# Attention over a cache and a gated layer on one core: values' products at the landing, output chunks shared by three engines

## The chip, the core and the metric

The kernel runs on one core of a Trainium2 chip: TensorE (PE), VectorE (DVE), ScalarE (ACT) and GpSimd (POOL) compute, SyncE (SP) issues nearly all transfers from HBM into SBUF. The metric is the device time of one execution in microseconds, the median of three runs.

## The reference

One token of decoding. `x` (576 numbers) is normalised; attention with 32 heads runs over a cache of 8192 keys and values of 128 numbers each, and a gated layer of width 4608 stands beside it.

```python
xn = _layernorm(x)
q = xn @ wq                                          # 32 heads x 128
p = softmax((q . k_cache) * 128 ** -0.5)             # 8192 per head
o = p . v_cache                                      # per head
a = concat(o) @ wo                                   # 4096 -> 576
g = xn @ W_gate;  g = g * (g > 0)
b = (g * (xn @ W_up)) @ W_down                       # 4608 -> 576
return x + a + b
```

All arrays are float32. Keys and values are 134 MB each, the four weights about 51 MB together.

## The kernel before

**Storage.** Most of SBUF is `slots`, three places of 128 x 16384 numbers: two for keys (`KEYS`), one for values (`VALUES`). A load of keys or values (`kk[i]`, `vv[i]`) fills one place with two heads (a pair; there are `NP` = 16). The weights of q, gate and up (`wl`, four tiles of 26 chunks of 576 columns) pass through the same places first, and the weights of both output products (`wod`, 68 chunks of 576 columns: 36 of `W_down`, 32 of `wo`) last. Pair p (from 1) has the keys `kk[p-1]` and the values `vv[p-1]`.

**Order.** Nothing is scheduled by a planner: `add(engine, f, waits, to)` appends to an engine's list, with the semaphores that it waits for and the one that it raises; `loop` and `done` enclose a hardware loop whose counter sets the waits' values. `emit` writes the lists. Each engine runs its list in order.

**Stages.** (1) x is broadcast to all partitions by a TensorE product with ones, normalised into `xp` (PSUM) and `xb` (SBUF). (2) The chunks of `wl` are multiplied with x and summed: most by VectorE (`dot`), 12 of each of the last three tiles by GpSimd (`others`) and ScalarE (`total`). The sums are columns of `dots`. (3) The loop over pairs. For each head VectorE multiplies the keys by q (`product`, in place) and adds up along a head's 128 numbers (`sums`), then takes the maximum per partition (`mr`). TensorE brings the maxima across partitions into `pm` (`maxima`), VectorE makes the negative bias `nb` (`bound`), ScalarE the exponentials (`soft`, with the sum of p into `L`), TensorE the products with the values (`values(0)`, `values(1)`, 16 matmuls each, into `bo`) and the sum of `L` over partitions (`pl`); ScalarE copies `bo` out (`oc`), four small matmuls turn it into `ot`, and `close` divides and writes columns of `coef`. A query for the next pair: GpSimd spreads columns of `dots` on a diagonal (`diagonals` into `dq`), and TensorE broadcasts it into `qb` (`query`). In this kernel each bias is computed half a pair late, between the next head's product and its sums, and the query stands between `values(0)` and `values(1)`. (4) The output: 62 chunks are added by VectorE alone into `acc` (60 in the loop at L380, two at L388), the last six (`LAST`) go through TensorE into `po` with `acc` itself; the two halves of the row are copied and stored.

**The queue on SP.** Keys of the next pair are asked for when the place is free (`sumb`) and the keys before have landed (`kland`); values when those of the pair before are used (`vb`). Increments on SP (`passed`, L157) tell other engines of a landing; `chunks` counts rounds of output chunks that are ready. An increment waits on the same queue as the loads do, so it also waits for whatever stands before it there.

Of the kernel before, what the change touches and what calls it, by code (L numbers as in the profile page):

```python
# [15 lines left out]
P = 128  # L16
# [21 lines left out]
LOADS = (27, 5, 4, 4, 4, 4, 4, 4, 4, 2, 2, 2, 1, 1)  # L38
ROUNDS = 15
LAST = 6  # L40

HEADS = {"tensor": 0, "vector": 128, "scalar": 128}


class Program:
# [21 lines left out]
    def loop(self, engine, start, end, step=1):  # L67
        self.lists[engine].append((start, end, step))
# [4 lines left out]
    def emit(self, engine):  # L73
        eng = getattr(self.nc, engine)
        lines = iter(self.lists[engine])
        if engine in HEADS:
            with self.nc.Fori(0, 1, 1, engines=[ENGINES[engine]], head_slot={ENGINES[engine]: HEADS[engine]}):
                self.run(engine, eng, lines, None)
        else:
            self.run(engine, eng, lines, None)  # L80

    def run(self, engine, eng, lines, counter):
        for line in lines:
            if line is None:
                return
            if len(line) == 3:
                with self.nc.Fori(*line, engines=[ENGINES[engine]]) as i:
# [12 lines left out]
def build(nc, x, wl, kk, vv, wod, out):  # L100
# [26 lines left out]
    acc = sb("acc", [P, D])  # L127
# [12 lines left out]
    mr = sb("mr", [P, 1])  # L140
    nb = [sb(f"nb{i}", [P, 1]) for i in range(2)]
    L = sb("l", [P, G])
    rl = sb("rl", [P, G])

    bo, bb, bm, bt, po = [bank(f"bank{i}") for i in range(5)]
    xp = nc.alloc_psum_tensor("xp", [P, 1024], F32).ap()[:, :D]
    qb = bb[:, :G * DH].rearrange("p (h d) -> p h d", d=DH)
    pm = bm[:, :P]
    ot = bt[:, :G]
    pl = bt[:, 8:8 + G]  # L150
# [34 lines left out]
    places, f = [], 0  # L185
    for k, n in enumerate(LOADS):
        if k == 1:
            load(VALUES, vv[NP - 1], (("vb", NP - 1),), "vland")
        waits = {0: (("sumb", NP - 1),), 1: (("sumb", NP),), 8: (("vb", NP),)}.get(k, ())
        load(slots[:, OUT + f * D:][:, :n * D], wod[:, f * D:(f + n) * D], waits, f"do{k}")  # L190
        f += n
        places += [k] * n
    assert f == H + FC
    ready = 0
    for k in range(max(places[:4 * ROUNDS]) + 1):
        full = sum(places[4 * m + 3] <= k for m in range(ROUNDS))
        if full > ready:
            passed(f"do{k}", "chunks", (full - ready))
            ready = full
# [9 lines left out]
    add("gpsimd", lambda e: e.memset(acc, 0.0), (), "acc0")  # L209
    add("gpsimd", lambda e: e.memset(pzs, 0.0), (), "pz0")  # L210
    def diagonals(pairs):
        for k in pairs:
            waits = (("q", k),) if k else (("dots", A + 3), ("scaled", 1))
            add("gpsimd", lambda e, k=k: e.tensor_mul(dq, scaled[:, None, :].to_broadcast([P, G, P]),  # L214
                                                      dots[:, G * k:G * k + G, None].to_broadcast([P, G, P])),
                waits, "dq" if k > 1 else "dq0")

    for k in range(3):
# [4 lines left out]
        if k == 0:  # L223
            diagonals(range(2))
    diagonals(range(2, NP))
    for k in range(2):
        add("gpsimd", lambda e: e.sem_inc(pr.sems["dq"], 1), (("q", NP + k),))

# [3 lines left out]

    add("scalar", lambda e: e.dma_start(xr, x), (), "dx", 16)
    mm((("dx", 16), ("ones", 1)), None, 0, xp[:, :512], ones[:1, :].to_broadcast([1, P]), xr[:, :512])
    mm((), "bx", 1, xp[:, 512:], ones[:1, :].to_broadcast([1, P]), xr[:, 512:])
# [5 lines left out]
    add("vector", lambda e: e.memset(pm, 0.0), (), "pmb", 1)  # L241
    add("vector", lambda e: e.memset(bt[:, :16], 1.0), (), "ot", 1)
    add("scalar", lambda e: e.activation(row, xp, AF.Copy, accum_out=sm[:, 0:1]), (("bx", 1),), "ln")  # L243
    add("vector", lambda e: e.tensor_scalar_mul(sm[:, 1:2], sm[:, 0:1], -1.0 / D), (("ln", 1),), "lv")  # L244
    add("vector", lambda e: e.tensor_scalar_add(xp, xp, sm[:, 1:2]), (("lv", 1),), "lv")
# [45 lines left out]

    def sums(m):
        x = "ab"[m]
        def f(e, i):
            k3 = slots[:, ds(at(i) + m * SK, SK)].rearrange("p (c d) -> p c d", d=DH)
            return e.reduce_sum(s2[m], k3, axis=AX.X)  # L296
        add("vector", f, (), f"sum{x}", 1)
        add("vector", lambda e, i: e.reduce_max(mr, s2[m], axis=AX.X), ((f"sum{x}", lambda i: i),), f"mr{x}", 1)  # L298


    def bound(m, value, waits=()):
        x = "ab"[m]
        add("vector", lambda e, *i: e.tensor_reduce(nb[m], pm, axis=AX.X, op=ALU.max, negate=True), waits + ((f"pm{x}", value),), f"nb{x}", 1)  # L303

    def close(value, place):
        add("vector", lambda e, *i: e.reciprocal(rl, pl), (("ot", value),), "rl", 1)
        add("vector", lambda e, *i: e.tensor_mul(coef[:, place(*i)], ot, rl), (("rl", value),), "os", 1)

    pr.loop("vector", 1, NP + 1)
# [8 lines left out]
    bound(1, NP + 1)  # L318
    add("vector", lambda e: e.tensor_copy(acc[:1, :], xr), (("acc0", 1), ("dx", 16)), "mrb")
    hh, gate, up = coef[:, :FC], dots[:, H:H + FC], dots[:, H + FC:]  # L320
    add("vector", lambda e: e.tensor_scalar(hh, gate, 0.0, None, op0=ALU.is_gt), (("sums", 3 * OTHERS), ("os", NP)), "mulb", 1)
    add("vector", lambda e: e.tensor_mul(hh, hh, gate), (("mulb", NP + 1),), "mra", 1)
    add("vector", lambda e: e.tensor_mul(hh, hh, up), (("mra", NP + 1),), "accd", 1)


    def soft(h):
        r, i = h // G, h % G
        waits = ((f"nb{'ab'[i]}", (r + 1 + i)),) + (((("va", r),) if r else (("pz0", 1),)) if i == 0 else ())
        add("scalar", lambda e: e.activation(pz[:, i, :, 4 * G - 4:4 * G], s2[i].rearrange("p (c b) -> p c b", b=4), AF.Exp,  # L329
                                             bias=nb[i], scale=1.0, accum_out=L[:, i:i + 1]), waits, f"exp{i}", 1)  # L330

    for r in range(NP):
        if r == 0:
            soft(0)
            soft(1)
        if r + 1 < NP:
            soft(G * r + G)
        add("scalar", lambda e: e.copy(row[:, :512], bo), (("vb", r + 1),), "oc", 1)  # L338
        if r + 1 < NP:
            soft(G * r + G + 1)  # L340
# [5 lines left out]
    def maxima(m, value):  # L346
        x = "ab"[m]
        mm(((f"mr{x}", value),), f"pm{x}", 1, pm, mr.to_broadcast([P, P]), ident)

    def values(i, waits):  # L350
        for c in range(C // 4):
            j = c % 4
            end = c == C // 4 - 1
            mm(waits if c == 0 else (), f"v{'ab'[i]}" if end else None, 1, bo[32 * j:32 * j + 4 * G, :],
# [3 lines left out]
    query((("dq0", 1),))  # L358
    maxima(0, 1)
    query((("dq0", 2), ("mulb", 1)))  # L360
    maxima(1, 1)
    pr.loop("tensor", 1, NP + 1)
    mm((("exp1", lambda i: i + 1),), None, 0, pl, ones.to_broadcast([P, P]), L)
    maxima(0, lambda i: i + 1)
    values(0, (("vland", lambda i: i * 16),))
    query((("dq", lambda i: i), ("mulb", lambda i: i + 1)))
    values(1, ())
    for b in range(4):
        mm((("oc", lambda i: i),) if b == 0 else (), "ot" if b == 3 else None, 1, ot, row[:, b * P:(b + 1) * P],
           sel.rearrange("p (i b) -> p i b", b=4)[:, :, b], b == 0, b == 3)  # L370
    maxima(1, lambda i: i + 1)
# [3 lines left out]

    pr.loop("vector", 1, ROUNDS + 1)
    for m in range(4):
        def chunk(e, i, m=m):
            c = slots[:, ds(i * (4 * D) + (OUT - 4 * D + m * D), D)]
            return e.scalar_tensor_tensor(out=acc, in0=c, scalar=coef[:, ds(i * 4 + (m - 4), 1)], in1=acc, op0=ALU.mult, op1=ALU.add)  # L380
        waits = ((f"acc{'dabc'[m]}", lambda i: i),) if m else (("chunks", lambda i: i), ("accd", lambda i: i))
        add("vector", chunk, waits, f"acc{'abcd'[m]}", 1)
    pr.done("vector")

    close(NP + 1, lambda: slice(FC + H - G, FC + H))
    for n, k in enumerate(range(4 * ROUNDS, H + FC - LAST)):
# [58 lines left out]
```

## Time and profile before

| | |
|---|---|
| median of three runs | 810.74 us (809.76 to 811.58) |
| the profiled execution's own time | 811.15 us |
| its span | 809.4 us |
| TensorE, share of the span | 27% |
| VectorE | 83% |
| ScalarE, GpSimd | 7% each |
| bytes moved by the queue on SP | 319.17 MB |

A time in the profile is in us from the start of the span; a line number (L289) is one of the kernel before. In a row of the timeline stand the start, the duration, the engine, the line, the operation with output and inputs, how many were merged, and in brackets the idle time before it with what ended it. In a row of stretches stand the busy time and count of PE, its weight loads, DVE, ACT and POOL, then the granted clock of TensorE, the transfers' share and GB/s.

### The profile page before, as it was taken

To read this page: it belongs to the slowest core of one execution; us is meant where nothing else is said; L and a number is where in the kernel's file an instruction comes from. 1 tells how busy PE (TensorE), PEld (TensorE's weight loads), DVE (VectorE), ACT (ScalarE), POOL (GpSimd) and SP (SyncE) were. 2 spreads that over 40 slices of the span, in tenths; PEclk is the share of its full clock that TensorE was granted. 3 is DMA by queue.
4 is the path that set the end of the run, shared out by engine and by line. 5 is a ranking of instruction groups with operands and counts; after the bars stand their busy time and mean duration, and the time that the engine had idled before them with its cause. 6 is when DMAs were issued, how large, how long until landed. Compare 5 with 4: busy or idle time off the path is not lost.

```text
span 809.4 us, 4277 instructions
## 1 busy us (share of the span) xinstructions
PE 221.1 (27%) x1320; PEld 76.4 (9%) x1320; DVE 674.0 (83%) x377; ACT 56.9 (7%) x161; POOL 56.2 (7%) x29
## 2 busy tenths in 40 slices
PE   1000001425050615233332324251505050605101
PEld 0000000111010101010101111110101010201000
DVE  1855599999999898989898989898989898903776
ACT  2025500000000000000000000000000000000000
POOL 0098400000000000000000000000000000000000
PEclk9999999958585757585756666665757575857555
DMA  9999999489999999999999999999999999999300
GB/s 387 453 432 440 424 418 415 207 363 440 440 415 463 418 415 466 415 421 460 415 460 421 415 466 415 415 466 415 428 453 415 463 418 415 445 415 421 124 0 0
DMA packets 7207, 319.20 MB, mean 394 GB/s; under 512 B 802, under 2 KB 802, under 8 KB 1444
## 3 DMA queue, kind: packets, MB, share of 16 engines
q1 hardware_dynamic: 7202, 319.17, 91.5%
q14 instruction: 2, 0.02, 0.0%
q8 instruction: 1, 0.02, 0.0%
q10 hardware_dynamic: 2, 0.00, 0.0%
HBM read 319.16 MB, written 0.00 MB: 394 GB/s over the span
## 4 chain that ended last, share of the span: by engine, by line
DMA 70%; DVE 19%; issue 4%; PE 3%; POOL 2%; DVEq 1%; ACTq 1%; SPq 1%; ACT 0%; POOLq 0%
DMA slots<-in_kk 65%; DVE slots L289 6%; DVE acc L380 6%; DVE s L296 5%; DMA slots<-in_vv 3%; PE bank L231 2%; POOL slots L221 2%; DMA xr<-in_x 1%; DVEq L380 1%; ACTq L281 0%; SPq L154 0%; PE xp L231 0%; SPq L180 0%; ACT slots L281 0%; DVE acc L388 0%
## 5 line engine op out<-in xcount | busy, mean ns | idle before, releaser
L289 DVE TENSOR_TENSOR slots<-slots,bank 128x8192 f32 x32 | 277.9, 8685 | 44.6 <-DMA slots<-in_kk 33.7
L296 DVE TENSOR_REDUCE s<-slots 128x64 f32 x32 | 277.6, 8674 | 0.0
L231 PE MATMUL bank<-slots,pzs 128*8 128x512 f32 x1024 | 147.2, 727 | 23.2 <-DMA slots<-in_vv 23.2
L231 PE MATMUL bank<-ident,mr 128*128 128x128 f32 x68 | 26.7, 495 | 225.8 <-DVE mr L298 225.8
L380 DVE SCALAR_TENSOR_TENSOR acc<-slots,coef,acc 128x576 f32<-128x576 f32 x60 | 49.1, 818 | 45.7 <-SPq L157 32.9
L259 DVE SCALAR_TENSOR_TENSOR slots<-slots,xp 128x576 f32 x68 | 46.2, 749 | 18.5 <-SPq L157 18.2
L231 PE MATMUL bank<-l,ones 128*128 128x2 f32 x32 | 9.4, 364 | 172.1 <-ACT pzs L329 172.1
L329 ACT ACTIVATE pzs<-s,nb 128x64 f32<-128x64 f32 x32 | 11.1, 348 | 527.5 <-DVE nb L303 527.5
L221 POOL TENSOR_TENSOR slots<-slots,xb 128x6912 f32<-128x6912 f32 x3 | 44.4, 14808 | 40.2 <-SPq L157 40.2
L214 POOL TENSOR_TENSOR dq<-scaled,dots 128x256 f32<-128x256 f32 x16 | 9.8, 616 | 523.4 <-PE bank L231 523.4
L231 PEld LDWEIGHTS bank<-slots,pzs 128*8 128x8 f32 x1024 | 27.8, 102 | 122.5 <-issue 95.2
L231 PEld LDWEIGHTS bank<-ident,mr 128*128 128x128 f32 x68 | 16.9, 308 | 229.8 <-DVE mr L298 229.8
L231 PE MATMUL bank<-dq,ones 128*128 128x256 f32 x36 | 13.1, 449 | 81.4 <-POOL dq L214 41.0
L281 ACT ACTIVATE slots<-slots x36 | 24.6, 683 | 53.7 <-POOL slots L221 53.7
L231 PEld LDWEIGHTS bank<-l,ones 128*128 128x128 f32 x32 | 8.0, 312 | 176.8 <-ACT pzs L329 176.8
L231 PE MATMUL bank<-sel,row 128*128 128x2 f32 x128 | 16.9, 254 | 11.3 <-ACT row L338 11.3
L231 PEld LDWEIGHTS bank<-sel,row 128*128 128x128 f32 x128 | 15.5, 191 | 26.1 <-ACT row L338 26.1
L338 ACT COPY row<-bank 128x512 f32<-128x512 f32 x16 | 9.4, 586 | 86.4 <-PE bank L231 86.4
L231 PEld LDWEIGHTS bank<-dq,ones 128*128 128x128 f32 x36 | 5.7, 200 | 96.5 <-issue 55.4
L231 PE MATMUL bank<-acc,ones 128*1 128x288 f32 x4 | 1.1, 664 | 47.8 <-DVE acc L388 47.8
L303 DVE TENSOR_REDUCE nb<-bank 128x1 f32<-128x128 f32 x33 | 9.6, 291 | 1.6 <-PE bank L231 0.5
L244 DVE TENSOR_SCALAR sm<-sm 128x1 f32<-128x1 f32 x1 | 0.2, 154 | 12.7 <-ACT row L243 12.7
(46 smaller groups left out, 57.2 us busy)
## 6 DMA issues: line engine op xcount, KB each, us to landing
slots<-in_wl SPq DMA_DIRECT2D x4, 7488.0 KB, 36.8
slots<-in_wod SPq DMA_DIRECT2D x7, 1152.0 KB, 31.8
slots<-in_wod SPq DMA_DIRECT2D x1, 7776.0 KB, 40.7
slots<-in_wod SPq DMA_DIRECT2D x3, 576.0 KB, 14.2
slots<-in_wod SPq DMA_DIRECT2D x1, 1440.0 KB, 24.8
slots<-in_wod SPq DMA_DIRECT2D x2, 288.0 KB, 15.5
slots<-in_kk SPq DMA_DIRECT2D x16, 38.3
slots<-in_vv SPq DMA_DIRECT2D x16, 26.7
```

The source lines that it names most:

```text
L214: add("gpsimd", lambda e, k=k: e.tensor_mul(dq, scaled[:, None, :].to_broadcast([P, G, P]), dots[:, G * k:G * k + G, None].to_broadcast([P ...
L221: return e.tensor_mul(c, c, xb[:, None, :].to_broadcast([P, OTHERS, D]))
L231: add("tensor", lambda e, *i: e.matmul(o, lhsT, rhs, start=start, stop=stop), waits, to, by)
L244: add("vector", lambda e: e.tensor_scalar_mul(sm[:, 1:2], sm[:, 0:1], -1.0 / D), (("ln", 1),), "lv")
L259: return e.scalar_tensor_tensor(out=c, in0=c, scalar=1.0, in1=xp, op0=ALU.mult, op1=ALU.mult, accum_out=dots[:, ds(column(i), 1)])
L281: return e.activation(c, c, AF.Copy, accum_out=dots[:, ds(within(t * MINE + i + (PER + MINE), PER + MINE, DOTS - 1), 1)])
L289: return e.tensor_mul(k3, k3, qb[:, m, None, :].to_broadcast([P, C, DH]))
L296: return e.reduce_sum(s2[m], k3, axis=AX.X)
L303: add("vector", lambda e, *i: e.tensor_reduce(nb[m], pm, axis=AX.X, op=ALU.max, negate=True), waits + ((f"pm{x}", value),), f"nb{x}", 1)
L329: add("scalar", lambda e: e.activation(pz[:, i, :, 4 * G - 4:4 * G], s2[i].rearrange("p (c b) -> p c b", b=4), AF.Exp, bias=nb[i], scale=1 ...
L338: add("scalar", lambda e: e.copy(row[:, :512], bo), (("vb", r + 1),), "oc", 1)
L380: return e.scalar_tensor_tensor(out=acc, in0=c, scalar=coef[:, ds(i * 4 + (m - 4), 1)], in1=acc, op0=ALU.mult, op1=ALU.add)
```

## The change

It has five parts, which the diff below shows cut to the core.

1. In the pair loop both heads' maxima come at the pair's end; one reduction makes both biases (`nb`), ScalarE does both exponentials in a loop, and TensorE's order is maxima, query, then all 32 products with the values.
2. x is broadcast by GpSimd (`partition_broadcast` into `xw`).
3. The sum of `L` over partitions is GpSimd's (`partition_all_reduce` into `lt`).
4. Output chunks go in 31 rounds of two: VectorE adds the first into `a0` (in PSUM), ScalarE scales the second in place, GpSimd adds it into `gs`. Two more are VectorE's, the last four TensorE's, with both sums. TensorE runs ten filler matmuls (`IDLE`) at rounds 26 to 30.
5. On SP the increments for landed chunks stand between the loads, the first right behind the load of the last values.

Also the loops around whole engines (`HEADS`) are gone, and the first of the last small loads are cut differently (`LOADS`).

```diff
-LOADS = (27, 5, 4, 4, 4, 4, 4, 4, 4, 2, 2, 2, 1, 1)
-ROUNDS = 15
-LAST = 6
-HEADS = {"tensor": 0, "vector": 128, "scalar": 128}
+LOADS = (27, 5, 4, 4, 4, 4, 4, 4, 4, 2, 2, 1, 1, 1, 1)
+ROUNDS = 31
+LAST = 4
+EARLY = 24
+IDLE = range(26, 31)
+HEAD = 0
...
+    output(LOADS[0])
+    load(VALUES, vv[NP - 1], (("vb", NP - 1),), "vland")
+    landed(0)
+    for n in LOADS[1:8]:
+        output(n)
+    for k in range(1, 5):
+        landed(k)
+    for n in LOADS[8:]:
+        output(n)
+    for k in range(5, len(LOADS)):
+        landed(k)
...
+    add("gpsimd", lambda e: e.partition_broadcast(xw, xr, P), (("dx", 16),), "bx")
...
+    pr.loop("gpsimd", 1, NP)
+    add("gpsimd", diagonals(lambda i: ds(i * G, G)), (("q", lambda i: i),), "dq")
+    add("gpsimd", lambda e, i: e.sem_inc(pr.sems["go"], 1), (("exp1", lambda i: i + 1), ("os", lambda i: i)))
+    add("gpsimd", lambda e, *i: e.partition_all_reduce(lt, L, P, bass.bass_isa.ReduceOp.add), (), "lt")
+    pr.done("gpsimd")
+    add("gpsimd", lambda e: e.sem_inc(pr.sems["dq"], 1), (("q", NP),))
+    add("gpsimd", lambda e, *i: e.partition_all_reduce(lt, L, P, bass.bass_isa.ReduceOp.add), (("exp1", NP + 1), ("os", NP)), "lt")
+    pr.loop("gpsimd", 1, ROUNDS + 1)
+    add("gpsimd", lambda e, i: e.tensor_add(gs, half(i), gs), (("halves", lambda i: i), ("gsum", lambda i: i)), "gsum")
+    pr.done("gpsimd")
...
     product(0, (("kland", lambda i: i * 16), ("q", lambda i: i)), "mula")
-    bound(1, lambda i: i, (("mula", lambda i: i), ("exp0", lambda i: i)))
     sums(0)
     product(1, (), "mulb")
-    bound(0, lambda i: i, (("mulb", lambda i: i), ("exp1", lambda i: i)))
     sums(1)
     close(lambda i: i, lambda i: ds(i * G + (FC - 2 * G), G))
+    add("vector", lambda e, i: e.tensor_reduce(nb, pm, axis=AX.X, op=ALU.max, negate=True), (("pm", lambda i: i),), "nb", 1)
...
+    for rounds in (range(1, EARLY + 1), range(EARLY + 1, ROUNDS + 1)):
+        pr.loop("scalar", rounds.start, rounds.stop)
+        add("scalar", lambda e, i: e.activation(half(i), half(i), AF.Copy, scale=coef[:, ds(i * 2 - 1, 1)]), (("chunks", lambda i: i),), "halves")
+        pr.done("scalar")
+        if rounds.start == 1:
+            rows(NP)
...
     pr.loop("tensor", 1, NP + 1)
-    mm((("exp1", lambda i: i + 1),), None, 0, pl, ones.to_broadcast([P, P]), L)
-    maxima(0, lambda i: i + 1)
-    values(0, (("vland", lambda i: i * 16),))
-    query((("dq", lambda i: i), ("mulb", lambda i: i + 1)))
+    maxima(0)
+    maxima(1)
+    query((("dq", lambda i: i + 1),))
+    values(0, (("vland", lambda i: i * 16), ("exp1", lambda i: i + 1)))
     values(1, ())
...
+    add("vector", chunk(lambda i: ds(i * (2 * D) + (OUT - 2 * D), D), lambda i: ds(i * 2 - 2, 1), a0, a0),
+        (("aa", lambda i: i), ("chunks", lambda i: i)), "aa", 1)
...
+    products((("gsum", ROUNDS + 1),), ones, gs, True)
     for k in range(H + FC - LAST, H + FC):
+        products(((f"do{places[k]}", 16),) + ((("os", NP + 1),) if k == H + FC - G else ()), coef[:, k:k + 1], slots[:, OUT + k * D:][:, :D], False, k == H + FC - 1)
+        if k == H + FC - 3:
+            products((("aa", n + 1),), ones, fs)
```

TensorE in the pair loop, before; the names in brackets are the semaphores waited for (`bank` is any of the PSUM places):

```order
L231 MATMUL bank<-l,ones 128x2 [waits s_exp1]
L231 MATMUL bank<-ident,mr 128x128 [waits s_mra]
L94 REGISTER_ALU
L231 MATMUL bank<-slots,pzs 8x512 [waits s_vland]
L231 MATMUL bank<-slots,pzs 8x512 x15
L231 MATMUL bank<-dq,ones 128x256 [waits s_mulb,s_dq]
L231 MATMUL bank<-slots,pzs 8x512 x16
L231 MATMUL bank<-sel,row 128x2 [waits s_oc]
L231 MATMUL bank<-sel,row 128x2 x3
L231 MATMUL bank<-ident,mr 128x128 [waits s_mrb]
```

The same loop on TensorE now:

```order
L252 MATMUL bank<-ident,mr 128x128 [waits s_mra]
L252 MATMUL bank<-ident,mr 128x128 [waits s_mrb]
L94 REGISTER_ALU
L252 MATMUL bank<-dq,ones 128x256 [waits s_dq]
L94 REGISTER_ALU
L252 MATMUL bank<-slots,pzs 8x512 [waits s_exp1,s_vland]
L252 MATMUL bank<-slots,pzs 8x512 x31
L252 MATMUL bank<-sel,row 128x2 [waits s_os,s_oc]
```

Both maxima and the query moved ahead of the products, which stand together and wait for both exponentials; the product with `l` is gone.

The end of the queue on SP, before (waits of increments are shown with the next transfer):

```order
L154 DMA slots<-in_vv 128x16384 [waits s_vb]
L154 DMA slots<-in_wod 128x2880 [waits s_sumb]
L154 DMA slots<-in_wod 128x2304 x6
L154 DMA slots<-in_wod 128x2304 [waits s_vb]
L154 DMA slots<-in_wod 128x1152 x3
L154 DMA slots<-in_wod 128x576 x2
L200 DMA out_y<-xb 1x576 [waits s_do0,s_do1,s_do2,s_do3,s_do4,s_do5,s_do6,s_do7,s_do8,s_end1,s_end0]
```

And now:

```order
L158 DMA slots<-in_vv 128x16384 [waits s_vb]
L158 DMA slots<-in_wod 128x2880 [waits s_do0,s_sumb]
L158 DMA slots<-in_wod 128x2304 x6
L158 DMA slots<-in_wod 128x2304 [waits s_do1,s_do2,s_do3,s_do4,s_vb]
L158 DMA slots<-in_wod 128x1152 x2
L158 DMA slots<-in_wod 128x576 x4
L215 DMA out_y<-xb 1x576 [waits s_do5,s_do6,s_do7,s_do8,s_do9,s_end1,s_end0]
```

The increments for the first landings (`do0`, and `do1` to `do4`) moved ahead of later loads; all of them stood behind the last load.

GpSimd from the pair loop to the end, now (before it had one `TENSOR_TENSOR` into `dq` per pair there and nothing at the end):

```order
L228 ISA
L228 TENSOR_TENSOR dq<-scaled,dots 128x256
L94 REGISTER_ALU
L241 ISA [waits s_exp1,s_os]
L241 ISA lt<-l 128x2
L87 REGISTER_ALU
L87 COMPARE_AND_BRANCH
L244 ISA lt<-l 128x2 [waits s_q,s_os,s_exp1]
L87 UNCONDITIONAL_BRANCH
L248 ISA [waits s_gsum,s_halves]
L248 ISA
L248 TENSOR_TENSOR xb<-slots,xb 128x576
```

`ISA` rows with an output are the partition operations. Ahead of the partition operations and of `TENSOR_TENSOR` the built program has an instruction that asks for the code library that holds them (one library for the former, another for the latter); in the last loop it stands in every round. In the kernel before, one such instruction stands ahead of the first `TENSOR_SCALAR_AFFINE_SELECT` (L204), and none after.

More of the change, by code (lines that the diff above doesn't have):

```diff
@@ L65, in add, with loop @@
         self.lists[engine].append((f, waits, to, by, first))
[L67 to L68 removed]
+    def loop(self, engine, start, end, step=1, head=None):
+        self.lists[engine].append((start, end, step, head))
     def done(self, engine):
@@ L73, in emit @@
     def emit(self, engine):
[L74 to L80, printed above, removed]
+        self.run(engine, getattr(self.nc, engine), iter(self.lists[engine]), None)
     def run(self, engine, eng, lines, counter):
@@ L332, in build @@
[L332 to L340, printed above, removed]
+    add("vector", lambda e: e.memset(a0, 0.0), (), "aa", 1)
+    add("vector", lambda e: e.tensor_scalar(hh, gate, 0.0, None, op0=ALU.is_gt), (("sums", 3 * OTHERS), ("os", NP)), "h0", 1)
+    add("vector", lambda e: e.tensor_mul(hh, hh, gate), (("h0", 1),), "h1", 1)
```

166 lines of the change are left out of this document (78 added, 88 removed).

## The prediction

> **What bounds the kernel now.** I read the page first (engines, slices), then stretches of the span, then the waits of VectorE and of the queue on SP, and the timeline around each wait. The page gives the shape:
>
> ```profile
> span 809.4 us, 4277 instructions
> PE 221.1 (27%) x1320; PEld 76.4 (9%) x1320; DVE 674.0 (83%) x377; ACT 56.9 (7%) x161; POOL 56.2 (7%) x29
> GB/s 387 453 432 440 424 418 415 207 363 440 440 415 463 418 415 466 415 421 460 415 460 421 415 466 415 415 466 415 428 453 415 463 418 415 445 415 421 124 0 0
> q1 hardware_dynamic: 7202, 319.17, 91.5%
> ```
>
> The bytes move at 415 to 466 GB/s in nearly every slice, whatever the engines do; the exceptions are slices 8 and 9 and the last three (of 20.2 us each). Stretches of the span, with the DMA share and GB/s as the last two columns, say how much is lost there:
>
> ```profile
> 150.40:164.20 13.80, 10.45 (x66) 2.07 (x58) 13.77 (x3) 0.55 (x3) 0.62 (x1) 0.88 0.01 5
> 205.00:670.00 465.00, 155.56 (x960) 53.91 (x960) 428.70 (x120) 17.61 (x60) 6.77 (x11) 0.65 1.00 433
> 754.00:756.00 2.00, 2.00 (x10) 0.51 (x8) 1.64 (x3) 0.00 (x0) 0.00 (x0) 0.50 0.47 173
> 755.00:809.40 54.40, 4.88 (x20) 0.90 (x16) 39.95 (x52) 0.39 (x1) 0.00 (x0) 0.54 0.00 0
> ```
>
> So three stages. From start to about 754.8 us transfers set the time (173 GB/s over 2 us is 0.8 us at 433), with a hole of 13.8 us at 150. After that 54.6 us pass without a byte. The floor, 319.17 MB at 433 GB/s, is 737 us.
>
> Why the last stage is long shows in VectorE's waits and its chunk loop:
>
> ```profile
> DVE acc L380 <- SPq L157: 32.9, 1, 32.9
> 740.78 0.82 DVE L380 SCALAR_TENSOR_TENSOR acc<-slots,coef,acc 128x576 f32<-128x576 f32 x1 [32.88 <-SPq L157]
> 741.79 0.82 DVE L380 SCALAR_TENSOR_TENSOR acc<-slots,coef,acc 128x576 f32<-128x576 f32 x1 [0.19 <-DVE acc L380]
> 744.94 0.82 DVE L380 SCALAR_TENSOR_TENSOR acc<-slots,coef,acc 128x576 f32<-128x576 f32 x1 [0.33 <-DVE acc L380]
> ```
>
> VectorE stood 32.9 us for SP's increment (L157), which stands on that queue behind the last weight loads, which wait for the last values' products. Then it did 60 chunks at 1.00 us each, 1.15 at a loop's turn: 0.18 is the wait for its own sum, 0.15 the turn.
>
> **The pairs, and the hole.** SP's issues and what starts on their landing:
>
> ```profile
> 164.22 0.36 SPq L182 DMA_DIRECT2D slots<-in_vv  x1
> 631.53 0.35 SPq L180 DMA_DIRECT2D slots<-in_kk  x1
> 650.57 5.46 PE L231 MATMUL bank<-slots,pzs 128*8 128x512 f32 x32 [0.36 <-DMA slots<-in_vv]
> 662.51 0.34 SPq L182 DMA_DIRECT2D slots<-in_vv  x1
> 670.19 8.69 DVE L289 TENSOR_TENSOR slots<-slots,bank 128x8192 f32 x1 [2.67 <-DMA slots<-in_kk]
> 689.27 4.88 PE L231 MATMUL bank<-slots,pzs 128*8 128x512 f32 x32 [0.37 <-DMA slots<-in_vv]
> ```
>
> Keys asked for at 631.53 land 19.6 us after the values before them, and values asked for at 662.51 land 19.1 us after those keys: loads (8.39 MB each, 19.4 us at 433 GB/s) land one after the other in the order of issue. A pair costs 38.7 us of transfer, and a late issue costs nothing while another load is under way. At 164.22 none was: values of pair 2 wait until those of pair 1 are used, and the second head's exponential waited for pair 2's first product. The head's half a pair of delay was harmless later, since the next keys were in flight.
>
> **Part 1: products at the landing.** Now both heads' maxima go to TensorE at the end of the pair, one reduction makes both biases, two exponentials follow, then the query, then all 32 products. VectorE's rows of the stage in which it sets the pace:
>
> ```profile
> 131.51 8.69 DVE L289 TENSOR_TENSOR slots<-slots,bank 128x8192 f32 x1 [0.61 <-issue]
> 140.23 0.29 DVE L303 TENSOR_REDUCE nb<-bank 128x1 f32<-128x128 f32 x1
> 140.44 8.67 DVE L296 TENSOR_REDUCE s<-slots 128x64 f32 x1
> 140.55 0.35 ACT L329 ACTIVATE pzs<-s,nb 128x64 f32<-128x64 f32 x1 [18.44 <-DVE nb L303]
> 167.05 0.16 DVE L306 RECIPROCAL rl<-bank 128x2 f32<-128x2 f32 x1
> 167.19 0.80 PE L231 MATMUL bank<-ident,mr 128*128 128x128 f32 x2 [1.41 <-DVE mr L298]
> 168.13 8.69 DVE L289 TENSOR_TENSOR slots<-slots,bank 128x8192 f32 x1 [0.60 <-issue]
> ```
>
> Pair 1's scores end at 130; plus 0.80 for the maxima, some 0.4 for the bias and 1.0 for two exponentials, the products can start about 132.5, where its values land too. Sixteen take 4.88 or 5.46 by the rows above (x32 counts their passes), thirty-two so about 10; the values of pair 2 are asked for near 142, while keys of pair 3 (issued 130.7) are still moving. The hole closes: -13.8. What is queued behind the new wait: VectorE's turn took 36.62 us (131.51 to 168.13); two reductions leave (2 x 0.21), the wait for the maxima, the joint reduction and the query add about 0.9, so 37.1. That is 1.6 under the 38.7 of transfer, so it costs nothing; without that cover each pair would pay the excess.
>
> **Part 2: x by GpSimd.** The first rows of ScalarE's and VectorE's work on x, and a dot beside GpSimd's product:
>
> ```profile
> 14.33 0.65 ACT L243 ACTIVATE row<-xp 128x576 f32<-128x576 f32 x1 [8.52 <-PE xp L231]
> 22.36 0.75 DVE L259 SCALAR_TENSOR_TENSOR slots<-slots,xp 128x576 f32 x1 [1.90 <-SPq L157]
> 40.99 0.75 DVE L259 SCALAR_TENSOR_TENSOR slots<-slots,xp 128x576 f32 x1
> ```
>
> The dots wait 1.90 for the first weights, x being long ready. GpSimd's copy waits for x's landing as TensorE's did; what it takes longer is covered by those 1.9, and past that by weight loads that are already queued: some us of late dots delay no transfer. Cost nothing.
>
> **Part 3: sum of p by GpSimd.** It needs one pair's time to arrive, being read a turn later; per pair GpSimd has one 0.6 us product and this. Nothing inside the loop. At the end it stands ahead of the chunk sums, and there it counts. Its price is in no row; nor is that of a change of GpSimd's code library, which the program asks for between partition operations and elementwise ones (and again, with the same library, in every round). GpSimd's and the nearest rows:
>
> ```profile
> 1.18 0.29 POOL L204 TENSOR_SCALAR_AFFINE_SELECT ident<-ident 128x128 f32<-128x128 f32 x1 [0.23 <-POOL ident L203]
> 39.86 14.78 POOL L221 TENSOR_TENSOR slots<-slots,xb 128x6912 f32<-128x6912 f32 x1 [36.92 <-SPq L157]
> 620.15 0.61 POOL L214 TENSOR_TENSOR dq<-scaled,dots 128x256 f32<-128x256 f32 x1 [38.08 <-PE bank L231]
> 16.91 1.28 ACT L247 ACT_TABLE_LOAD   x1
> 1.26 10.60 DMA xr<-in_x
> ```
>
> Partition sum: between 0.29 and 14.78, the ends of GpSimd's rows; its two columns are nearest to the 0.61 of 256, so 0.6. Change of library: the ask ahead of L204 fits in that row's 0.23 us with a semaphore's wait, so a repeated one is cheap; a real change I put at 1.3, the nearest row of an engine that loads a table, with 0.1 below and 10.6 above (a small transfer in loaded queues, as x's was).
>
> The Trainium skill, GPSIMD Engine Reference, section 2.1, Instruction dispatch, says that the first call into a freshly loaded kernel pays about 6 us for loading its code (5.95 measured); no run here shows one. By it the sum below would be 4.7 higher, an estimate.
>
> **Part 4: chunks in rounds of two.** Per round VectorE adds one chunk (1.15), ScalarE scales the other (0.65 by its row at 14.33, about 1.0 with a turn), GpSimd adds that. GpSimd: from 256 to 6912 elements 0.61 goes to 14.78, so 2.13 ns an element and 1.30 for 576. With the 0.23 for the wait on its own sum and the repeated ask, 1.53 a round; with a turn of 0.15 like VectorE's, 1.68. Without any it can't be under 1.30. I take 1.53: the registers of a turn can be done beside the running sum. The 31 rounds take 47.4 on GpSimd against 35.7 on VectorE, so GpSimd is the slower leg. VectorE's sum is now in PSUM, as x was in its dots, whose 0.75 was the same without GpSimd (22.36) and beside it (40.99). Clearing it and the gate's products come before the first chunks land: nothing.
>
> **Part 5: the queue on SP.** The increments now stand between loads. The first is behind the last values' load only. The last seven loads stand behind the fourth landing: those 17 chunks (0.68 us each) land 11.6 us after the last values, the 29 queued chunks last 19.7, and seven issues take 3:
>
> ```profile
> 739.06 0.43 SPq L154
> ```
>
> Margin 5 us, cost nothing; without it the transfers would stop.
>
> **The sum**, on the profiled run's clock:
>
> ```profile
> 705.60 0.22 DVE L298 TENSOR_REDUCE mr<-s 128x1 f32<-128x64 f32 x1
> 707.03 0.35 ACT L329 ACTIVATE pzs<-s,nb 128x64 f32<-128x64 f32 x1 [5.36 <-DVE nb L303]
> 804.59 1.13 PE L231 MATMUL bank<-acc,ones 128*1 128x288 f32 x4 [47.76 <-DVE acc L388]
> 805.50 2.13 PE L231 MATMUL bank<-slots,coef 128*1 128x288 f32 x8
> 807.68 0.45 DVE L401 COPY xb<-bank 1x288 f32<-1x288 f32 x1 [3.15 <-PE bank L231]
> ```
>
> Last keys land at 670.19 - 13.8 = 656.4. Scores of pair 16 end 35.2 later (705.82 - 670.19, less 2 x 0.21): 691.6. Maxima to the first exponential about 1.4 more, the exponentials 1.1: 694.1, and the first 27 chunks, next behind the values that land at 689.27 (8.0 MB, 18.4), are there at 689.27 + 18.4 - 13.8 = 693.9. Partition sum 0.6, library 1.3: 696.0. GpSimd's rounds 47.4: 743.4. TensorE has this sum ahead of everything else in its order, so all six products of 1x576 follow it: 24 passes where 12 took 3.07 (804.59 to 807.66), 6.1 at the clock of then, since I don't count on the ten filler products of rounds 26 to 30 to last until 743: 749.5. Copy, store and end as before 1.7 (807.66 to 809.4): 751.2. The profiled run took 811.15, so 1.75 lies around the span: 753. That is 58 under 811.15 (and 811.15 is 0.4 over the median of 810.74, which is within what the runs scatter).
>
> **Rivals.** (a) GpSimd keeps up and the transfers set the end. For: its rounds with 1.30 would end at 736. Against: the wait on its own sum. The last bytes land at 754.8 - 13.8 = 741.0, then four passes (1.1), 1.7, 1.75: 745.5.
> (b) The library's code comes late, by a transfer in loaded queues. For: x's small load took 10.60. Against: the 0.23 at L204. With 10.6 for 1.3, and 1.68 a round (+4.6), 753 + 9.3 + 4.6 = 767; in the loop two changes are 21 of the 36 us there, still hidden.
> The skill's sentence above is the middle of this rival: with it alone about 758.
> (c) Slower than before: the repeated ask in GpSimd's round costs a load each time. It decides from (811 - 753) / 31 = 1.9 more a round; at 10.6 it would be some 1,080. Against it stands the 0.23 alone, which holds one such ask.
> (d) The pair loop becomes VectorE's: 13 turns, each with what passes 1.6 of extra. Two us extra a turn end at 758; the sign would change only above 6.
>
> **Chances.** Likeliest 753 (between 749 and 758, with the rounds from 1.45 to 1.68): 50%. (a), 744 to 748: 22%. (b), with the skill's figure in it, 758 to 770: 20%. (c) 4%, (d) 3%; that an order undoes both gains and leaves the time as it was, 1%. The range from 744 to 767 leaves out (c) and the ends. The runs scatter by 0.2% (809.76 to 811.58), which is also about what can be told from no change: faster 0.94, same 0.01, slower 0.05.
>
> **What would show it.** Stretch 150 to 164 at about 433 GB/s; bytes ending near 741; VectorE's first chunk near 695; keys' pitch still 38.7; GpSimd's adds 1.5 apart and ending within a few us of 743; TensorE's last wait on GpSimd's sum. Wrong if the adds are more than 1.9 apart, if a gap of over 5 us stands before the first, if the queue on SP stops the bytes near 725 to 735, or if VectorE's turn passes 38.7.

## Result and profile after

The changed kernel takes 799.1 us (median of four runs, 796.93 to 800.09) beside 811.16 for the kernel before (809.76 to 811.69): a ratio of 0.985, with a 95% interval from 0.9825 to 0.9876. That is 12 us or 1.5% less, which the interval sets apart from no change but which is under the 2% that is called faster here; 58 us were forecast, and the result lies 32 above the upper end of the range. The profiled execution took 800.09 with a span of 797.9; the forecast's sum had 751.2 for the span, so 46.7 us have to be found.

The page of the changed kernel, the lines that answer to those shown of before:

```profile
span 797.9 us, 4973 instructions
PE 209.7 (26%) x1294; PEld 67.2 (8%) x1294; DVE 650.6 (82%) x331; ACT 94.7 (12%) x206; POOL 107.7 (13%) x78
GB/s 384 432 432 446 425 453 375 414 421 421 457 404 430 375 453 388 421 381 453 388 411 427 414 427 411 421 424 378 434 407 421 421 414 404 419 421 397 407 194 0
q1 hardware_dynamic: 7346, 319.17, 94.5%
```

The two weak slices (207 and 363 GB/s) are gone, and the stretch without a byte at the end is down from 54.6 to some 24 us; yet the ordinary slices are lower: 375 to 430 is frequent where 415 to 466 was the rule. Stretches of the span (DMA share and GB/s last) show three things:

```profile
150.40:164.20 13.80, 0.79 (x2) 0.50 (x2) 13.58 (x4) 0.00 (x0) 0.61 (x1) 0.50 1.02 437
283.00:670.00 387.00, 115.03 (x718) 36.57 (x722) 346.22 (x89) 24.55 (x58) 10.12 (x20) 0.60 0.98 415
766.00:768.00 2.00, 2.00 (x7) 0.59 (x5) 1.65 (x2) 1.40 (x2) 1.68 (x2) 0.56 0.90 340
768.00:770.00 2.00, 2.00 (x11) 0.76 (x9) 0.89 (x2) 1.25 (x2) 1.68 (x2) 1.00 0.11 43
770.00:772.00 2.00, 0.84 (x4) 0.17 (x2) 1.70 (x4) 0.94 (x2) 1.68 (x2) 1.00 0.10 34
772.00:774.00 2.00, 0.00 (x0) 0.00 (x0) 1.68 (x3) 0.00 (x0) 1.68 (x2) 1.00 0.06 23
```

The hole at 150 is closed. In the pair loop 415 GB/s pass instead of 433. And the transfers end in a tail: from 768 to 774 the DMA share is 0.11, 0.10, 0.06, which is one or two of the core's 16 transfer engines still at work when the others have finished (one of 16 is 0.06).

VectorE's waits for keys in the changed kernel (in all, times, longest), then its timeline: GpSimd and ScalarE at the end of pair 1 and in pair 12, VectorE's starts on the keys of pairs 14 to 16, then the end.

```profile
DVE slots L306 <- DMA slots<-in_kk: 33.1, 9, 4.6
134.19 0.33 ACT L343 ACTIVATE pzs<-s,nb 128x64 f32<-128x64 f32 x1
145.56 0.41 POOL L241 PARTITION_ALL_REDUCE lt<-l  x1 [53.05 <-issue]
158.12 0.61 POOL L228 TENSOR_TENSOR dq<-scaled,dots 128x256 f32<-128x256 f32 x1 [12.14 <-issue]
573.10 0.41 POOL L241 PARTITION_ALL_REDUCE lt<-l  x1 [27.67 <-issue]
587.26 0.60 POOL L228 TENSOR_TENSOR dq<-scaled,dots 128x256 f32<-128x256 f32 x1 [13.75 <-issue]
605.68 8.69 DVE L306 TENSOR_TENSOR slots<-slots,bank 128x8192 f32 x1 [3.56 <-DMA slots<-in_kk]
646.07 8.69 DVE L306 TENSOR_TENSOR slots<-slots,bank 128x8192 f32 x1 [3.54 <-DMA slots<-in_kk]
687.18 8.69 DVE L306 TENSOR_TENSOR slots<-slots,bank 128x8192 f32 x1 [4.57 <-DMA slots<-in_kk]
724.64 0.19 ACT L343 ACTIVATION_READ_ACCUMULATOR pzs<-s,nb 128x1 f32 x1
724.93 0.40 POOL L244 PARTITION_ALL_REDUCE lt<-l  x1 [30.55 <-ACT pzs L343]
737.96 1.39 POOL L248 TENSOR_TENSOR xb<-slots,xb 128x576 f32<-128x576 f32 x1 [12.63 <-issue]
741.66 1.40 POOL L248 TENSOR_TENSOR xb<-slots,xb 128x576 f32<-128x576 f32 x1 [0.33 <-POOL xb L248]
789.88 1.40 POOL L248 TENSOR_TENSOR xb<-slots,xb 128x576 f32<-128x576 f32 x1 [0.32 <-POOL xb L248]
791.33 1.13 PE L252 MATMUL bank<-xb,ones 128*1 128x288 f32 x4 [20.48 <-POOL xb L248]
796.28 0.45 DVE L417 COPY xb<-bank 1x288 f32<-1x288 f32 x1 [22.57 <-PE bank L252]
```

"issue" in brackets means that the engine waited for nothing that the profile shows. Read so, GpSimd shows a gap of 10 to 14 us at every passage from one kind of operation to the other in the pair loop: the last exponential of pair 1 ends at 134.52 and the partition sum that waits for it starts at 145.56; from that sum's end to the product `dq` pass 12.1 us, at 573 13.75, and at the end of the kernel 12.63 before the first chunk sum. The operations are short, 0.41 and 0.6. At each of these passages the built program asks for the other code library, so I take the gaps for the changes of library. In the loop nothing on VectorE waits for GpSimd. But in its last nine turns VectorE waits 3.2 to 4.6 us for keys, and its last starts on them are 40.4 apart (605.68 to 646.07) and 41.1 (646.07 to 687.18), where the transfers' own rate would make it 38.7.

How a load lands says more. Each of the 16 transfer engines moves a part and adds one to the load's semaphore. The time from the first to the last of these increments, worked out from the trace's landing events for successive loads of keys in the pair loop, in us:

```
before             1.6, then 0.4 to 0.5 throughout
after              4.2 6.2 8.5 10.5 10.5 9.7 9.3 9.1 8.9 10.1 10.5 9.7 9.7 9.9
```

In the kernel before all parts land together. In the changed one the spread grows by some 2 us with each pair up to the fourth load and then stays near 10, and the load counts as landed with its last part. Sorted by time, the 16 increments of one load show how many parts are late; for the keys of pair 16, in us after the first:

```
before             0.0 0.0 0.0 0.1 0.1 0.1 0.1 0.2 0.2 0.2 0.2 0.2 0.2 0.2 0.3 0.4
after              0.0 0.0 0.1 0.2 0.2 0.2 0.2 0.3 0.3 0.4 0.5 0.6 4.2 4.3 4.7 9.9
```

Twelve parts land as before, three some 4 us later and one 10. The other loads in the loop look alike: it is four parts of the sixteen that lag, one of them most. The theory from this: the changes of library, not the sums themselves, slow the transfers. Its rivals: only the change at the end counts; ScalarE's table loads do it; the partition sums do it.

### The profile page after: what moved, and what is told of

It is laid out like the page before. It is cut to its first block, busy times and chain, and to the rows that moved or that the text cites. A ratio compares the mean times of both kernels' runs of the same rounds, so it can differ in the third digit from the quotient of the medians.

```text
span 797.9 us, 4973 instructions
## 1 busy us (share of the span) xinstructions
PE 209.7 (26%) x1294; PEld 67.2 (8%) x1294; DVE 650.6 (82%) x331; ACT 94.7 (12%) x206; POOL 107.7 (13%) x78
## 2 busy tenths in 40 slices
DMA packets 7351, 319.20 MB, mean 400 GB/s; under 512 B 818, under 2 KB 818, under 8 KB 1588
## 4 chain that ended last, share of the span: by engine, by line
DMA 58%; DVE 26%; issue 6%; POOL 5%; PE 1%; SPq 1%; ACTq 1%; ACT 0%; POOLq 0%; DVEq 0%
DMA slots<-in_kk 49%; DVE s L314 13%; DVE slots L306 13%; DMA slots<-in_wod 9%; POOL xb L248 3%; POOL slots L233 2%; PE bank L252 1%; SPq L158 1%; ACTq L298 0%; SPq L184 0%; ACT slots L298 0%; ACTq L87 0%; DVE mr L318 0%; POOLq L248 0%; DVEq L306 0%
## 5 line engine op out<-in xcount | busy, mean ns | idle before, releaser
L252 PE MATMUL bank<-ident,mr 128*128 128x128 f32 x64 | 20.6, 415 | 216.3 <-DVE mr L318 216.3
L241 POOL PARTITION_ALL_REDUCE lt<-l x15 | 6.1, 407 | 427.0 <-issue 427.0
L276 DVE SCALAR_TENSOR_TENSOR slots<-slots,sum 128x576 f32 x68 | 46.2, 749 | 19.8 <-SPq L161 19.5
L248 POOL TENSOR_TENSOR xb<-slots,xb 128x576 f32<-128x576 f32 x31 | 43.5, 1403 | 22.5 <-issue 12.6
L393 DVE SCALAR_TENSOR_TENSOR sum<-slots,coef,sum 128x576 f32<-128x576 f32 x32 | 26.3, 823 | 21.1 <-SPq L161 15.0
L252 PEld LDWEIGHTS bank<-ident,mr 128*128 128x128 f32 x64 | 13.1, 255 | 220.4 <-DVE mr L318 220.4
L358 ACT ACTIVATE slots<-slots,coef x31 | 21.7, 767 | 24.0 <-SPq L161 24.0
L252 PE MATMUL bank<-dq,ones 128*128 128x256 f32 x34 | 17.8, 625 | 25.9 <-POOL dq L228 25.9
L330 DVE TENSOR_REDUCE nb<-bank 128x2 f32<-128x256 f32 x16 | 6.8, 425 | 7.6 <-PE bank L252 7.6
```

What stands on the lines that cost most here:

```text
L248: add("gpsimd", lambda e, i: e.tensor_add(gs, half(i), gs), (("halves", lambda i: i), ("gsum", lambda i: i)), "gsum")
L252: add("tensor", lambda e, *i: e.matmul(o, lhsT, rhs, start=start, stop=stop), waits, to, by)
L276: return e.scalar_tensor_tensor(out=c, in0=c, scalar=1.0, in1=xp, op0=ALU.mult, op1=ALU.mult, accum_out=dots[:, ds(column(i), 1)])
L358: add("scalar", lambda e, i: e.activation(half(i), half(i), AF.Copy, scale=coef[:, ds(i * 2 - 1, 1)]), (("chunks", lambda i: i),), "halves")
L393: return lambda e, *i: e.scalar_tensor_tensor(out=to, in0=slots[:, place(*i)], scalar=coef[:, factor(*i)], in1=acc, op0=ALU.mult, op1=ALU.add)
```

## The experiments

All "before" medians beside these runs were 809.67 or 809.55 us (seven runs each).

**1. The sum of p back on TensorE, all else as in the change.** It takes away every library change but the two for x's broadcast, and the repeated ask in the rounds with them. Theory A: the changes slow the transfers and stand in the tail. Theory B: only the tail's change counts.

```diff
-    add("gpsimd", lambda e, *i: e.partition_all_reduce(lt, L, P, bass.bass_isa.ReduceOp.add), (), "lt")
...
-    add("gpsimd", lambda e, *i: e.partition_all_reduce(lt, L, P, bass.bass_isa.ReduceOp.add), (("exp1", NP + 1), ("os", NP)), "lt")
...
-    values(0, (("vland", lambda i: i * 16), ("exp1", lambda i: i + 1)))
+    mm((("exp1", lambda i: i + 1), ("os", lambda i: i)), "lt", 1, lt, ones.to_broadcast([P, P]), L)
+    values(0, (("vland", lambda i: i * 16),))
```

> The changed kernel with the sum of p over partitions on TensorE again (one matmul with ones per pair, ahead of the values' products); GpSimd has no partition operation in the pair loop or after it, so no change of code library there. Theory A (each change of library brings code by one transfer engine, which then lags, and every load waits for it): the keys' pitch falls from 40.3 to 38.7 us, the last keys land near 659 instead of 687, the 12.6 us ahead of GpSimd's first chunk sum go: about 759 us. Rival B (the table loads that ScalarE now has in every pair, 1.28 us each, hold the transfers up): they stay here, so the pitch stays at 40.2 and only the 12.6 us go: about 787 us.

Measured: 760.4 us (760.33 to 761.33), ratio to before 0.9399 (0.9384 to 0.9415). First a stretch of the span, then the timeline: VectorE's start on pair 16, the end of its second exponential, and GpSimd at the start and the end of the rounds:

```profile
283.00:670.00 387.00, 128.94 (x806) 45.35 (x806) 366.76 (x95) 27.17 (x64) 6.12 (x10) 0.62 1.00 434
```

```profile
661.61 8.69 DVE L302 TENSOR_TENSOR slots<-slots,bank 128x8192 f32 x1 [0.80 <-PE bank L248]
699.09 0.19 ACT L339 ACTIVATION_READ_ACCUMULATOR pzs<-s,nb 128x1 f32 x1
701.09 1.40 POOL L244 TENSOR_TENSOR xb<-slots,xb 128x576 f32<-128x576 f32 x1 [76.73 <-ACT slots L354]
702.75 1.41 POOL L244 TENSOR_TENSOR xb<-slots,xb 128x576 f32<-128x576 f32 x1 [0.26 <-POOL xb L244]
750.54 1.40 POOL L244 TENSOR_TENSOR xb<-slots,xb 128x576 f32<-128x576 f32 x1 [0.24 <-POOL xb L244]
```

A holds, with a time 1.4 over the 759 expected: 38.7 of the 46 us between 753 and 799.1 hang on who adds up `L`. The loop moves 434 GB/s again and the spread of landings is 0.6 us for every load of keys in it.

**2. No partition operation at all**: experiment 1 with x broadcast by TensorE as before.

```diff
-    add("gpsimd", lambda e: e.partition_broadcast(xw, xr, P), (("dx", 16),), "bx")
+    mm((("dx", 16), ("ones", 1)), None, 0, xp[:, :512], ones[:1, :].to_broadcast([1, P]), xr[:, :512])
+    mm((), "bx", 1, xp[:, 512:], ones[:1, :].to_broadcast([1, P]), xr[:, 512:])
```

> As the kernel before this one in the call, and x is broadcast by TensorE again: no library change at all. Theory A: the first keys land 2 us earlier (94.9 instead of 97.0), pitch 38.7, about 757 us. Rival B: about 785 us.

Measured: 759.11 us (758.54 to 759.51), 1.3 less than experiment 1; the runs of the two don't overlap. So part 2 of the change costs little here. VectorE's waits (in all, times, longest) and its timeline in pair 16 show what sets the pace once the transfers are undisturbed:

```profile
DVE slots L303 <- PE bank L247: 11.9, 15, 0.8
```

```profile
659.82 8.69 DVE L303 TENSOR_TENSOR slots<-slots,bank 128x8192 f32 x1 [0.80 <-PE bank L247]
695.13 0.22 DVE L315 TENSOR_REDUCE mr<-s 128x1 f32<-128x64 f32 x1
```

VectorE waits for the query (0.8 at the most, in 15 turns), never for keys: its turns of 37.64 follow one another from the first pair. The keys of pair 16 land at 655.99 by the landing events (656.4 was forecast), and VectorE starts on them at 659.82.

**3. The kernel before, with library changes and nothing else**: in each of pairs 2 to 15 GpSimd does a partition sum of a constant that nobody reads. It adds 27 changes to a kernel whose loop has none: 14 to the sums' library and 13 back (the expectation counts one too many).

```diff
-    diagonals(range(2, NP))
+    for k in range(2, NP):
+        diagonals([k])
+        add("gpsimd", lambda e: e.partition_all_reduce(spare, two, P, bass.bass_isa.ReduceOp.add), (("two", 1 + k - 2),), "two")
```

> The kernel before, with a partition sum of a constant put on GpSimd after each pair's diagonal (14 of them, so 28 changes of library); nothing reads its result. Theory A: the keys' pitch goes from 38.7 to about 40.2 us and the last keys land some 25 us later, the time is about 835 us. Rival B (no table load is added): pitch 38.7, about 811 us.

Measured: 829.2 us in one run, 19.5 more than before; about 835 was expected. A stretch of the span, then GpSimd's timeline:

```profile
283.00:670.00 387.00, 120.33 (x734) 42.20 (x738) 342.31 (x98) 13.65 (x47) 9.61 (x19) 0.62 0.99 419
```

```profile
606.51 0.41 POOL L229 PARTITION_ALL_REDUCE spare<-two  x1 [9.02 <-issue]
...
645.62 0.41 POOL L229 PARTITION_ALL_REDUCE spare<-two  x1 [8.09 <-issue]
```

The chain of waits has the loads of keys, with the time of the start:

```profile
569.54 39.70 DMA slots<-in_kk
...
609.59 39.60 DMA slots<-in_kk
```

Nothing waits for the sum, no other engine has another order, and the loop still falls from 433 to 419 GB/s; keys are 40.05 apart (569.54 to 609.59). VectorE's waits in this run name no wait for the query. The last keys land at 688.49 by the landing events instead of 669.87: 18.6 of the 19.5.

One change of this run fell into the hole of the kernel before, where no load was under way. A stretch of the span, then GpSimd's timeline:

```profile
156.00:165.00 9.00, 6.18 (x37) 1.58 (x37) 8.96 (x3) 1.03 (x3) 0.62 (x1) 0.81 0.00 0
158.88 0.62 POOL L216 TENSOR_TENSOR dq<-scaled,dots 128x256 f32<-128x256 f32 x1 [24.33 <-PE bank L235]
165.58 0.41 POOL L229 PARTITION_ALL_REDUCE spare<-two  x1 [6.08 <-issue]
```

It took 6.08 us, where the other thirteen to this library took 8.09 to 10.79 beside the loads. By this one instance the loads delay the changes, as the changes delay the loads.

**4. ScalarE's table loads.** Its pair loop now loads a table in every turn (1.28 us, 15 times), which the kernel before did not do. The rival: these loads come through the transfers too. The loop is written out, and the table stays.

```diff
-    pr.loop("scalar", 1, NP)
-    soft(lambda i: i)
-    rows(lambda i: i)
-    pr.done("scalar")
+    for i in range(1, NP):
+        soft(i)
+        rows(i)
```

> The changed kernel with ScalarE's pair loop written out, so that its 15 table loads fall to one. Theory A: as the changed kernel, about 799 us, pitch 40.2. Rival B: pitch 38.7, about 770 us.

Measured: 798.6 us in one run, within the runs of the changed kernel, and the loop is no faster:

```profile
283.00:670.00 387.00, 114.18 (x734) 35.91 (x738) 347.76 (x87) 12.98 (x49) 10.08 (x20) 0.61 0.98 413
```

ScalarE is busy 11.6 us less there, and 413 GB/s move instead of 415. The table loads are acquitted.

**5. The change or the operation?** Experiment 3 with four partition sums in a row per pair: the same 27 changes, four times the operations.

```diff
-        add("gpsimd", lambda e: e.partition_all_reduce(spare, two, P, bass.bass_isa.ReduceOp.add), (("two", 1 + k - 2),), "two")
+        for j in range(4):
+            add("gpsimd", lambda e: e.partition_all_reduce(spare, two, P, bass.bass_isa.ReduceOp.add), (("two", 1 + 4 * (k - 2) + j),), "two")
```

> The kernel before with four partition sums of a constant behind each other per pair, where the earlier run had one: four times the operations, the same 28 changes of library. Theory A (the change costs, not the operation): 829 us as with one, keys' pitch 40.0. Rival (the partition operation itself disturbs the transfers): the added 20 us become some 80, about 890 us.

Measured: 824.45 us in one run, not more than with one sum. The same two views:

```profile
283.00:670.00 387.00, 123.27 (x756) 42.24 (x756) 346.23 (x95) 13.64 (x47) 21.52 (x49) 0.63 0.99 422
```

```profile
643.09 1.88 POOL L230 PARTITION_ALL_REDUCE spare<-two  x4 [9.35 <-issue]
```

Four sums take 1.88 us, with one gap of 9.35 ahead of them all. What costs is the passage from one library to the other. The spread of landings over the runs (us, successive loads of keys) goes the same way:

```
experiment 1 and 2   0.6 throughout
experiment 6         2.2, then 0.6 throughout
experiment 7         0.5 to 0.6 throughout
experiment 8         1.9 to 2.1 throughout (one part)
experiment 3         3.1 0.9 3.3 5.1 6.3 7.3 8.0 7.7 7.8 8.3 6.8 6.4 6.9 6.6
experiment 4         2.2 3.9 6.4 8.8 10.6 11.5 11.0 10.3 10.0 9.7 9.8 9.9 9.8 9.3
four sums            1.8 1.8 3.6 5.2 6.4 6.7 7.0 6.6 6.0 6.8 7.4 7.1 6.2 5.7
```

Of the kernels listed (6 to 8 follow below), each that changes libraries in the loop has a growing spread, most of it in four late parts, and none that doesn't.

**6. The increments on SP alone**: the kernel before with part 5 of the change only, to see what that part was worth by itself.

```diff
+            landed(0)
+        if k == 8:
+            for m in range(1, 5):
+                landed(m)
...
-    for k in range(max(places[:4 * ROUNDS]) + 1):
-        full = sum(places[4 * m + 3] <= k for m in range(ROUNDS))
-        if full > ready:
-            passed(f"do{k}", "chunks", (full - ready))
-            ready = full
+    for k in range(5, max(places[:4 * ROUNDS]) + 1):
+        landed(k)
```

> The kernel before with only the queue on SP changed: the increments for landed chunks stand between the loads as in the changed kernel. VectorE's 32.9 us wait ahead of the chunks goes, everything behind it moves up by 32 us: about 779 us. If the chunks' landing rather than the increment held VectorE (rival), it gains under 10 us.

Measured: 778.87 us in one run, 30.7 less than before, as expected. The first chunk starts early:

```profile
708.51 0.82 DVE L386 SCALAR_TENSOR_TENSOR acc<-slots,coef,acc 128x576 f32<-128x576 f32 x1 [0.35 <-DVE coef L329]
```

It started at 740.78 before. This part alone gains more than the whole change as it was made.

**7. A better split of the end.** With the partition operations gone (experiment 2), GpSimd's rounds still end the kernel. They become 24 instead of 31, TensorE takes eight of the last chunks, and GpSimd's sum is taken up ahead of the last two chunks' products.

```diff
-ROUNDS = 31
-LAST = 4
+ROUNDS = 24
+LAST = 8
-EARLY = 24
+EARLY = 20
-IDLE = range(26, 31)
+IDLE = range(20, 25)
...
-    products((("gsum", ROUNDS + 1),), ones, gs, True)
...
+            products((("gsum", ROUNDS + 1),), ones, gs)
```

> The kernel without partition operations (759 us), with GpSimd's share cut from 31 chunks to 24 and TensorE's raised from 4 to 8; VectorE takes the rest, and GpSimd's sum goes into the product later. If GpSimd's sum is what is left to wait for (it ended 9 us after the last landing), its end moves from 750 to about 739, the last bytes set the end near 741, and the time is about 748 us. If VectorE or TensorE is as late (rival), it stays at 755 to 759.

Measured: 749.89 us (749.51 to 750.13), ratio 0.9267 (0.9252 to 0.9283). GpSimd's last add and TensorE's last wait:

```profile
737.18 1.40 POOL L243 TENSOR_TENSOR xb<-slots,xb 128x576 f32<-128x576 f32 x1 [0.24 <-POOL xb L243]
738.84 4.97 PE L247 MATMUL bank<-slots,coef 128*1 128x288 f32 x24 [7.40 <-DMA slots<-in_wod]
```

TensorE's products now wait for the last weights, not for GpSimd, and from there TensorE's passes run to the final copy: the transfers, with those passes behind them, set the end.

**8. The query earlier**: experiment 7 with the query between the two heads' maxima, to take VectorE's wait of 0.8 out of each turn.

```diff
     maxima(0)
+    query((("dq", lambda i: i + 1), ("mulb", lambda i: i)))
     maxima(1)
-    query((("dq", lambda i: i + 1),))
```

> The same with the query ahead of the second head's maxima, where it waits for the second product only. VectorE's turn should fall from 37.6 by the 0.8 us that it waits for the query, its scores end some 3 to 4 us earlier (the keys land then), and where the end hangs on the last bytes the time is the same as the kernel before it in the call, 748; if it hangs on the chunk sums, 745.

Measured: 749.75 us (749.1 to 750.43), ratio 0.9262 (0.9246 to 0.9277): no gain. VectorE's turn falls from 37.64 to 37.16, by 0.48 and not 0.8, and from pair 13 on the time so gained is a wait for keys:

```profile
581.23 8.69 DVE L303 TENSOR_TENSOR slots<-slots,bank 128x8192 f32 x1 [1.86 <-DMA slots<-in_kk]
```

Of the kernels tried these two are the fastest, some 49 us under the change as it was made and 60 under the kernel before.

## Why the prediction was wrong

**The step that failed is part 3**, the sentence "Nothing inside the loop", and with it rival (b)'s "in the loop two changes are 21 of the 36 us there, still hidden". The changes are hidden for GpSimd and for all who wait for it. They are not hidden for the transfers, in a kernel whose time is transfers. The forecast priced the change on the engine that makes it and asked only who waits for that engine; it didn't ask what the code travels through, though rival (b) rests on just that, a load of code in loaded queues.

By the forecast's own sum, with the rows after:

| term | forecast | measured | difference |
|---|---|---|---|
| second exponential of pair 16 ends | 694.1 | 724.8 | +30.7 |
| from there to GpSimd's first add: partition sum and library | 1.9 | 13.2 | +11.3 |
| GpSimd's 31 rounds | 47.4 | 53.3 | +5.9 |
| TensorE's 24 passes | 6.1 | 5.0 | -1.1 |
| copy, store and end | 1.7 | 1.6 | -0.1 |
| sum | 751.2 | 797.9 | +46.7 |

- **The last exponentials, +30.7.** VectorE starts on the last keys at 687.18 instead of 656.4. In experiment 1, without the changes in the loop, the exponentials end at 699.28 (699.09 and 0.19): 25.5 of the 30.7 are the library changes'. The other 5.2 are there without them, in experiment 1. They are VectorE's: the size of its turn was right (37.64 measured, 37.1 forecast), but "1.6 under the 38.7 of transfer, so it costs nothing" was not. Closing the hole moves the transfers 13.8 us ahead and leaves VectorE's start where it was, so VectorE, not the keys, sets the pace: from the first pair to the last in experiments 1 and 2, and for the first seven pairs in the change as made, until the lagging loads overtake it. A turn that is shorter than the transfer makes up the lag only by the difference per pair; at pair 16 3.4 us were left in experiment 2 (659.82 against 656.4), and in experiment 1, whose first pair starts 1.8 later with x by GpSimd, 5.2 (661.61).
- **The library at the end, +11.3.** Taken as 1.3, from a table load of ScalarE; measured 12.6. The upper bound, 10.6 from the small load of x in loaded queues, was the nearer neighbour; that code, too, is a small transfer behind large ones fits the 6.08 of experiment 3 in the hole, but no record shows its bytes. The Trainium skill, GPSIMD Engine Reference, section 2.1, Instruction dispatch, says that new code can come to GpSimd by a DMA, that its first call pays about 6 us, and that no instruction shows it in the profile. The trace agrees that nothing shows but a gap, and with the figure where no load was under way: 6.08 us in experiment 3. Beside the loads the gap is 8.1 to 13.75, up to more than twice the page's figure, and it comes at every change; the measurement decides.
- **The rounds, +5.9.** 1.73 apart ((789.88 - 737.96) / 30) instead of 1.53, nearer to rival (b)'s 1.68. The add takes 1.40, not 1.30 as a line through 256 and 6912 elements gave, and the wait between two is 0.32 instead of 0.23. In experiment 1, whose rounds hold no ask for a library, it is 0.24: the repeated ask costs 0.08 a round, 2.5 in all. Rival (c), a load in each round, is excluded.
- **What held.** The hole closed, at 437 GB/s. x by GpSimd cost 1.3 us between experiments 1 and 2; in the change as made it was not taken away alone. The early increments alone are worth 30.7 us (experiment 6), and the queue on SP did not stop the bytes. TensorE's last wait was for GpSimd's sum. Bytes were to end near 741 and ended at 774 with the lagging loads; in experiment 1, without the changes in the loop, they end near 743.
- **Of the rivals**, (b) had the late library in the tail and nearly its size (10.6 for 12.6), and failed in the loop; (a), transfers setting the end, holds in experiments 7 and 8 only: 749.9 and 749.8, where it said 745.5. (d) asked for a turn of VectorE above 38.7, which did not come; VectorE set the pace with a shorter one. With the library changes of the loop and the end away, the change as made (experiment 1: 760.4) lies 7 over the forecast and inside its range, the 5.2 of VectorE and the longer rounds being left.

## What to carry to other kernels

A GpSimd operation from another library is not priced by its own 0.4 us, nor by who waits for GpSimd: in a kernel that lives on transfers, count the changes of library per turn of the loop and take each as a delay of the loads themselves (in experiment 3, 19.5 us for 27 changes), or put the work on an engine that needs no change. When loads land later than their bytes explain, look at the spread of a load's increments and at the last slices with a DMA share of one or two sixteenths: they show a few lagging parts that a mean GB/s hides. And when a hole in the transfers is closed, work out from its own start where the next engine's chain of turns ends, not only whether one turn is shorter than the transfer.

## What the runs showed of the hardware

- A change of GpSimd's code library took 8.1 to 13.75 us beside the loads, 12.6 at the end of the kernel, and 6.08 in the one case where no load was under way (experiment 3). A repeated ask for the resident one cost 0.08.
- Two changes per pair made four of a load's 16 parts land late, by some 2 us more with each of the first pairs, up to 10.5 us in the changed kernel, 11.5 in experiment 4 and 8.3 in experiment 3; 413 to 422 GB/s moved instead of 434.
- The partition sum of 128x2 itself takes 0.41 us, four in a row 1.88, and x's broadcast to 128 partitions 0.87, by this row of the changed kernel's timeline:

```profile
12.30 0.87 POOL L225 PARTITION_BROADCAST xw<-xr  x1 [10.23 <-issue]
```

- ScalarE's table loads (1.28 each, one per pair) did not slow the transfers.

Shown is that the changes make the loads land late, by experiments 1, 3, 4 and 5. Inferred is that the code passes through a few of the 16 transfer engines, ahead of or among their parts of the loads. The late increments speak for four of them, not for the one that the expectation of experiment 1 supposes, but the increments do not name their engine, and the bytes of the code are not in the records (319.20 MB in the kernel before and in the changed one). Why the spread stops at some 10 us is open too; it fits that the fast engines then have no more loads to run ahead with, since a pair's next values are asked for only when those before are used. A partition sum made with operations of the library that the rest uses was not tried.
